# A Hyena convolution with a gated layer behind it: work that TensorE waits for at changes of stage queued earlier, and the first x * v as whole products

## Chip, core and metric

The kernel runs on one core of a Trainium2 chip. The metric is the device time of one execution in microseconds (us). The kernel before takes 3784.62 us, the median of three runs (3782.5 to 3785.52). The profile shows one further execution, with a span of 3782.9 us.

## What is computed

Four batches of 12480 positions and 128 channels. A small network makes a filter from the position embeddings; each channel of u = x * v is convolved with it by a Fourier transform of twice the length; the result times x goes through a wide layer with the gate h * cos(h).

```python
h_mlp = np.maximum(pos_emb @ w1, 0.0) @ w2
h_filt = h_mlp * np.exp(-0.01 * pos)[:, None]
u = x * v
Uf = np.fft.rfft(u, n=L, axis=1)              # L = 2 * S
Hf = np.fft.rfft(h_filt, n=L, axis=0)
y = np.fft.irfft(Uf * Hf[None, :, :], n=L, axis=1)[:, :S, :]
x = (x * y).reshape(B * S, D)                 # 49920 x 128
h = x @ w_in                                  # 128 -> 2048
out = (h * np.cos(h)) @ w_out                 # 2048 -> 128
```

## The kernel before

The Fourier transform is done as matmuls in two factors, 96 (`N1`) by 120 (`N2`). The stages of a convolution are called f1 (first factor, 64 pairs of channels), f2 (second factor, 48 units of two frequencies, with the product with the filter's spectrum), i1 and i2 (the two factors back). Batches 1 to 3 run their convolution between the matmuls of the wide layer, which fills the kernel from about 343 us on. The change concerns what comes before: the filter and the convolution of batch 0, which have TensorE to themselves.

The order of instructions on each engine is written out by hand (`manual_schedule`): each engine works through its own queue in the order in which the Python code records the instructions, and waits at the first whose inputs or buffers are not ready. Generators (`units`) record a stage in small steps; interleaving two of them with `next` sets what stands where in the queues. In `units`, `before(j)` records what unit j needs `ahead` units early, `mm` its matmuls, and `after(j)`, a generator, is stepped through while the next unit is recorded.

The stages of the first 340 us, in TensorE's order:

- The hidden layer of the filter, eleven blocks (lines 831 to 841). VectorE scales a block (`filter_scale`, L333), TensorE turns it and multiplies, ScalarE evicts. `first_u` begins here: x and v of batch 0 are loaded in 30 units, multiplied (`u_multiply`, L392), and folded into `slots` by one sum on GpSimd and one difference on VectorE (`u_sums`, L398). A unit is 104 rows by 512 numbers, multiplied in two halves of 256; `engine(j, half)` says by whom. x has three buffers and v two.
- The filter's output (`filter_out`): 30 steps of two matmuls (L354), a copy by ScalarE (L358) and two sums by VectorE (L361) into `ftile`, with `first_u` beside it.
- f1 of the filter (`f1_units` with `f1_evict_filter`): 64 matmul pairs (L404), each evicted either by ScalarE or by VectorE (L431 to L434, and the negated copies L412 and L414). `share` is the part that ScalarE takes. The remaining steps of `first_u` run beside the first part of it. Then the tables of the inverse transform are made beside it (`inverse_tables`): ten sine tables, the arguments by GpSimd (L200 to L217), the sines by ScalarE (L226), recorded up to four tables later.
- f1 of batch 0 (`f1_evict`: L420, L422, L412 and L414), in place in `slots`. Beside it eight pieces of the wide layer's input weights are converted from 64-bit numbers (`convert_units`, L133 to L156) by VectorE, ScalarE and GpSimd.
- f2 of batch 0 and of the filter together (`f2_both_units`). For each unit ScalarE and VectorE make a table w (`make_w`, L291 and L293), two buffers of which lie in the pool `both`; TensorE multiplies w with the data (L445) and with the filter (L448, L451); ScalarE scales the filter's spectrum to h (L624, three buffers); VectorE makes two products of 512 (L464) and GpSimd joins them (L471). h and w are stored to DRAM by SyncE (L626, L613) for the later batches.
- i1 (`i1_units`: L476, evicted by a ScalarE copy L484 and two VectorE sums L486). Beside it eight pieces of the output weights are converted, and six groups of a table for i2 are made and stored (`some_groups`).
- i2 with the first step of the wide layer. `next(backs[0])` records the first group of the i2 table (`make_group`, tile `tm`).

The eight PSUM banks are handed out in turn by `bank()`, so TensorE may run up to eight banks ahead of the evictions.

## Time and profile before

| part of the page or the trace | value |
|---|---|
| time, median of 3 | 3784.62 us |
| busy: TensorE, VectorE, ScalarE, GpSimd | 98%, 73%, 67%, 69% of the span |
| hidden layer of the filter | 0 to 31 us |
| filter output: TensorE; VectorE ends | 31 to 57 us; 63.1 us |
| f1 of the filter, TensorE | 63.2 to 112.7 us |
| GpSimd: last sum of u; tables | 95.8 us; 96.3 to 119.1 us |
| f1 of batch 0, TensorE | 120.6 to 164.8 us |
| f2, TensorE | 169.5 to 267.7 us |
| i1, TensorE | 271.7 to 331.7 us |
| first matmul of i2 | 336.6 us |
| TensorE busy from 345 to 3780 us | 3406.5 of 3435 us |

A line of the trace's timeline gives start, duration, engine, line of the code, operation, the tiles out and in, the number of instructions merged, and in brackets the idle time of the engine before it with what ended it. A line of the list of waits gives who waited for whom, the total, how many times and the longest. A line L201 of the kernel before is not L201 of the one after: all lines here are those of before.

### The profile page before, as it was taken

How to read it: one execution, taken by the hardware profiler on the slowest of the kernel's cores; microseconds unless marked ns; L12 is line 12 of the kernel's file. 1: busy time of each engine (PE TensorE's matmuls, PEld its weight loads, DVE VectorE, ACT ScalarE, POOL GpSimd, SP SyncE). 2: the span in 40 equal slices, each digit the busy share in tenths (PEclk: the TensorE clock that was granted, in tenths of full speed). 3: DMA queues.
4: the chain of work that ended last, by engine and by line, in shares of the span. 5: the costliest groups of instructions: out<-in, count | busy, mean ns of one | idle time of the engine just before them, and what ended most of it. 6: DMA issues, size and time to landing. Idle time of an engine off the chain costs nothing.

```text
span 3782.9 us, 47199 instructions
## 1 busy us (share of the span) xinstructions
PE 3701.9 (98%) x13546; PEld 2107.3 (56%) x13546; DVE 2762.4 (73%) x5562; ACT 2520.3 (67%) x4683; POOL 2592.6 (69%) x2342
## 2 busy tenths in 40 slices
PE   7898999999999999999999999999999999999999
PEld 6777555655466555555565556555566544444444
DVE  7887887688866777778766786788765566666666
ACT  5756776766665557666665567666664677777777
POOL 7667886588854665688745664788644577777776
PEclk9999999999999999999999999999999999999999
DMA  5263552022202650122103540122105200000000
GB/s 166 69 179 106 149 147 57 18 70 79 74 18 67 179 159 27 33 78 78 57 18 110 173 127 18 51 78 76 41 12 167 87 20 20 17 21 20 17 22 13
DMA packets 209498, 276.14 MB, mean 73 GB/s; under 512 B 17111, under 2 KB 146535, under 8 KB 209111
## 3 DMA queue, kind: packets, MB, share of 16 engines
q1 hardware_dynamic: 209239, 273.12, 24.7%
q8 instruction: 109, 1.79, 0.2%
q14 instruction: 150, 1.23, 0.1%
HBM read 193.64 MB, written 79.42 MB: 72 GB/s over the span
## 4 chain that ended last, share of the span: by engine, by line
PE 83%; POOL 6%; DVE 3%; DMA 3%; ACT 2%; issue 2%; SPq 0%; POOLq 0%; DVEq 0%; ACTq 0%
PE ph L737 32%; PE acc L762 27%; PE cv L762 5%; PE cv L501 4%; PE cv L476 4%; POOL f L746 4%; PE cv L404 3%; PE cv L445 3%; PE ph L126 2%; DMA hd<-h 2%; PE ps L404 1%; POOL tm L297 1%; DMA tm<-td 1%; DVE k L743 1%; ACT cs L751 1%
## 5 line engine op out<-in xcount | busy, mean ns | idle before, releaser
L746 POOL TENSOR_TENSOR f<-a,k 128x512 f32<-128x512 f32 (+1 forms) x1568 | 1987.4, 1268 | 1054.2 <-DVE k L743 1052.0
L737 PE MATMUL ph<-at,w_in_sb 128*128 128x512 f32 (+1 forms) x3136 | 1600.2, 592 | 5.8 <-DVE gt L753 5.2
L740 ACT ACTIVATE a<-ph,quarter 128x512 f32<-128x512 f32 (+1 forms) x1568 | 1073.4, 685 | 760.5 <-PE ph L737 751.0
L762 PE MATMUL acc<-gt,w_out_sb 128*128 128x512 f32 (+1 forms) x2688 | 1374.1, 593 | 9.7 <-ACT ot L768 9.3
L753 DVE TENSOR_TENSOR gt<-ph,cs 128x512 f32<-128x512 f32 (+1 forms) x1568 | 1077.3, 687 | 318.5 <-ACT cs L751 288.9
L743 DVE TENSOR_SCALAR k<-a 128x512 f32<-128x512 f32 (+1 forms) x1568 | 768.5, 490 | 623.4 <-ACT a L740 601.6
L751 ACT ACTIVATE cs<-f 128x512 f32<-128x512 f32 (+1 forms) x1568 | 980.3, 625 | 330.6 <-POOL f L746 328.1
L762 PEld LDWEIGHTS acc<-gt,w_out_sb 128*128 128x128 f32 x2688 | 505.6, 189 | 662.8 <-issue 619.5
L737 PEld LDWEIGHTS ph<-at,w_in_sb 128*128 128x128 f32 x3136 | 554.0, 190 | 338.7 <-issue 269.5
L471 POOL TENSOR_TENSOR slots<-slots,t 120x256 f32<-120x256 f32 x384 | 311.4, 817 | 58.7 <-DVE t L464 26.0
L501 PEld LDWEIGHTS cv<-slots,tm 96*104 96x104 f32 x1920 | 241.0, 171 | 110.7 <-issue 83.0
L501 PE MATMUL cv<-slots,tm 96*104 96x128 f32 x1920 | 255.6, 275 | 10.4 <-DVE tm L293 4.9
L762 PE MATMUL cv<-gt,w_out_sb 128*128 128x512 f32 (+1 forms) x448 | 224.5, 583 | 0.7 <-DVE gt L753 0.7
L476 PEld LDWEIGHTS cv<-cs,slots 120*96 120x96 f32 x1536 | 176.7, 167 | 67.6 <-issue 65.7
L476 PE MATMUL cv<-cs,slots 120*96 120x120 f32 x1536 | 183.1, 266 | 0.0
L445 PE MATMUL cv<-slots,w 124*120 124x256 f32 x576 | 173.0, 380 | 0.0
L445 PEld LDWEIGHTS cv<-slots,w 124*120 124x120 f32 x576 | 103.6, 184 | 123.8 <-issue 111.1
L404 PEld LDWEIGHTS cv<-c,slots 104*124 104x124 f32 x768 | 132.5, 192 | 71.2 <-issue 58.3
L404 PE MATMUL cv<-c,slots 104*124 104x192 f32 x768 | 151.2, 326 | 4.8 <-DVE gt L753 3.5
L762 PEld LDWEIGHTS cv<-gt,w_out_sb 128*128 128x128 f32 x448 | 84.9, 190 | 104.5 <-issue 99.5
L392 DVE TENSOR_TENSOR xt<-xt,vt 104x256 f32<-104x256 f32 x177 | 138.3, 788 | 0.4 <-DMA vt<-in_v_dram 0.4
L486 DVE TENSOR_TENSOR slots<-cv,other 96x240 f32<-96x240 f32 x384 | 133.7, 394 | 4.2 <-ACT other L484 4.2
(129 smaller groups left out, 2564.1 us busy)
## 6 DMA issues: line engine op xcount, KB each, us to landing
h<-hd SPq DMA_DIRECT2D x144, 240.0 KB
tm<-td SPq DMA_DIRECT2D x96, 312.0 KB
xt<-in_x_dram SPq DMA_DIRECT2D x120, 208.0 KB
vt<-in_v_dram SPq DMA_DIRECT2D x120, 208.0 KB
xs<-in_x_dram SPq DMA_DIRECT2D x120, 208.0 KB
zd<-zs SPq DMA_DIRECT2D x119, 208.0 KB
zb<-zd SPq DMA_DIRECT2D x96, 256.0 KB
w<-wd SPq DMA_DIRECT2D x144, 116.2 KB
```

Of the source, the lines that this page charges most:

```text
L404: nc.tensor.matmul(ps[0:KE, i * 2 * N1:(i + 1) * 2 * N1], u[:, b, 0:KE, i], c1[0:u.shape[0], :, :].rearrange("p r k -> p (r k)"), start=Tr ...
L445: nc.tensor.matmul(pi, w[:, i, :], parts[0:KE, :, k], start=True, stop=True)
L471: nc.gpsimd.tensor_tensor(y[:, r], y[:, r], t[:, r], op=op)
L476: nc.tensor.matmul(ps[0:N1, (i * 2 + r) * N2:(i * 2 + r + 1) * N2], parts[0:N2, r, :, b, i], cs[:, r, :], start=True, stop=True)
L501: nc.tensor.matmul(ps[0:R, i * D:(i + 1) * D], t[:, i, r, :], slots[0:N1, :, place, :], start=(r == 0), stop=(r == 1))
L737: nc.tensor.matmul(ph[:, 0:m], w_in_sb[:, c * P:(c + 1) * P], ats[n][:, 0:m], start=True, stop=True)
L740: nc.scalar.activation(a[:, 0:m], ph[:, 0:m], AF.Identity, bias=quarter[:, 0:1], scale=INV_TWO_PI)
L743: nc.vector.tensor_scalar(out=k[:, 0:m], in0=a[:, 0:m], scalar1=ROUND, scalar2=ROUND, op0=ALU.add, op1=ALU.subtract)
L746: nc.gpsimd.tensor_tensor(f[:, 0:m], a[:, 0:m], k[:, 0:m], op=ALU.subtract)
L751: nc.scalar.activation(cs[:, 0:m], f[:, 0:m], AF.Sin, scale=TWO_PI)
L753: nc.vector.tensor_tensor(gt[:, 0:m], ph[:, 0:m], cs[:, 0:m], op=ALU.mult)
L762: nc.tensor.matmul(accs[n][:, 0:m], w_out_sb[:, c, :], gt[:, 0:m], start=(c == 0), stop=(c == NFC - 1))
```

## The change

It is meant to have ready, when TensorE comes to a new stage, what that stage's first matmul needs, and to even out who does x * v of the first batch:

- x * v of batch 0: one product of 512 a unit. GpSimd does it, except for units 15, 19, 23 and 27, which VectorE does. `first_u` is a unit of two steps, not three: one from the third block of the hidden layer on, two in each three steps of the filter output, and three steps of f1 to each of the rest.
- ScalarE takes 58% of the filter's f1 evictions, not 53%.
- The tables of the inverse run on into f1 of batch 0 (`chain`), and their last four sines are recorded one by one.
- The first w of f2 is made before f1 of batch 0 goes on; the buffers of w get a pool of their own. Stores of w are recorded behind the store of h.
- The last unit of f2 joins its products on VectorE, not GpSimd.
- Conversions: one in 9 and 10 steps, not 14; the groups of tables beside i1 one in 4, not 5; the first i2 table is made before the last of the six groups.

```diff
-        t.finish(len(t.waiting))
+        while t.waiting:
+            t.finish(1)
+            yield
...
-                for half in range(2):
+                for half in (0, 1) if halves else (slice(0, 2),):
                     u_multiply(tiles[j], half, engine(j, half))
                     yield
...
-    def f2_both_units(bank):
+    def f2_both_units(bank, w_pool):
+        ws, unkept = {}, []
+        def before(j):
+            ws[j] = w_pool.tile([KE, 2, N2], F32, name="w")
+            for i in range(2):
+                make_w(ws[j][:, i, :], 2 * j + i, half=bank)
+            unkept.append(j)
...
             nc.sync.dma_start(hd[j, :, :, :, :], h[:, :, :, :])
+            while unkept:
+                k = unkept.pop(0)
+                nc.sync.dma_start(wd[k, :, :, :], ws[k][:, :, :])
+            yield from f2_product(pool, ps[0], h, 2 * j, True,
+                                  nc.vector if 2 * j + 2 == N1 else nc.gpsimd)
...
-                nc.sync.dma_start(wd[j, :, :, :], ws[j][:, :, :])
...
-        next(backs[0])
+            if g == SOME[-2]:
+                next(backs[0])
...
-                                  lambda j, half: nc.vector if half and j % 3 and j < 18
-                                  else nc.gpsimd)
+                                  lambda j, half: nc.vector if j >= 15 and j % 4 == 3
+                                  else nc.gpsimd, halves=False)
...
-                    if i >= 4:
-                        for _ in range(2):
-                            next(first_u)
+                    if i >= 2:
+                        next(first_u)
...
-                    for _ in range(1 + (j % 3 == 0)):
+                    if j % 3:
                         next(first_u)
-            f1 = f1_units(bank, ftile[0:FR, :, :, :], 0.53, f1_evict_filter)
+            f1 = f1_units(bank, ftile[0:FR, :, :, :], 0.58, f1_evict_filter)
             for _ in first_u:
-                for _ in range(2):
+                for _ in range(3):
                     next(f1)
...
-                for i, _ in enumerate(f1):
-                    if i % 5 == 0:
-                        next(sines, None)
-                for _ in sines:
-                    pass
+                first_f1 = f1_units(bank, slots[0:R, :, :, :], 0.55)
+                for i, _ in enumerate(chain(f1, first_f1)):
+                    if i % 5 == 0 and next(sines, "made") == "made":
+                        break
...
-                        if i % 14 == 0:
+                        if i % every == 0:
                             next(convert, None)
-                        elif i % 5 == 0:
+                        elif i % 4 == 1:
                             next(other, None)
...
+            w_pool = first.enter_context(tc.tile_pool(name="w", bufs=2, side="right"))
+            f2 = f2_both_units(bank, w_pool)
+            next(f2)
+            beside(first_f1, [(wind[:, c], w) for c, w in in_pieces], 9)
...
-            beside(i1_units(bank), [(w_out_sb[:, c, :], w) for c, w in out_pieces], some_groups)
+            beside(i1_units(bank), [(w_out_sb[:, c, :], w) for c, w in out_pieces], 10, some_groups)
```

## Prediction

> **What bounds the kernel now.** I read the page's slices first, then the busy time of each stage, then TensorE's waits, then the timeline at each change of stage. From 345 us on TensorE is busy 3406.5 of 3435 us, in an order that the change leaves as it is; only the convolution of the first batch, the first 340 us, can move. Here is busy time by stage (length, then PE, PEld, DVE, ACT, POOL, granted clock, DMA share, GB/s):
>
> ```profile
> 31.00:63.00 32.00, 25.84 (x120) 19.23 (x118) 29.63 (x83) 11.05 (x30) 26.84 (x32) 0.96 0.59 175
> 63.00:96.00 33.00, 31.53 (x177) 30.60 (x178) 30.64 (x95) 24.88 (x110) 29.68 (x39) 0.94 0.51 148
> 96.00:113.00 17.00, 15.14 (x83) 12.99 (x82) 16.43 (x63) 12.06 (x52) 14.06 (x39) 1.00 0.03 7
> 113.00:120.60 7.60, 0.56 (x4) 0.27 (x2) 4.69 (x17) 2.02 (x8) 5.24 (x12) 0.85 0.11 33
> 120.60:165.00 44.40, 43.99 (x252) 43.06 (x252) 38.70 (x105) 39.10 (x115) 28.76 (x31) 0.95 0.24 69
> 165.00:169.50 4.50, 0.01 (x1) 0.04 (x1) 1.66 (x6) 4.39 (x16) 0.72 (x1) 1.00 0.18 52
> 169.50:267.70 98.20, 95.87 (x480) 74.50 (x480) 83.56 (x189) 53.17 (x141) 64.28 (x91) 0.98 0.59 172
> 267.70:271.70 4.00, 0.45 (x2) 0.25 (x2) 1.83 (x3) 0.60 (x1) 3.65 (x6) 1.00 0.63 189
> 271.70:331.70 60.00, 55.58 (x510) 54.33 (x510) 45.44 (x141) 38.85 (x120) 41.31 (x54) 0.97 0.27 85
> 331.70:336.60 4.90, 0.02 (x1) 0.02 (x1) 4.69 (x16) 4.33 (x14) 3.31 (x6) 0.67 0.10 27
> ```
>
> I call them filter output (31-63), f1 of the filter (63-113), f1 of batch 0 (120.6-165), f2 (169.5-267.7) and i1 (271.7-331.7). TensorE's idle time lies between them, in waits that the list of waits names (total, times, longest):
>
> ```profile
> PE ps L404 <- ACT slots L412: 8.1, 4, 7.1
> PE ps L404 <- DVE ftile L361: 6.3, 1, 6.3
> PE cv L501 <- DVE tm L293: 4.9, 1, 4.9
> PE ps L445 <- DVE w L293: 6.4, 4, 4.7
> PE ps L476 <- POOL slots L471: 3.6, 2, 3.4
> ```
>
> These five longest waits add to 26.4 us, 0.7% of the kernel. But VectorE is 93 to 97% busy in the f1 stage of the filter, and 87% in that of batch 0 with a start that waits, so a gap can close without a stage ending sooner. The timeline shows what is behind two of them:
>
> ```profile
> 119.11 0.30 ACT L226 ACTIVATE tw_t<-turned 96x120 f32<-96x120 f32 x1 [1.89 <-POOL turned L217]
> 123.59 0.55 DVE L420 COPY slots<-ps 64x384 f32<-64x384 f32 x1 [5.75 <-PE ps L404]
> 173.23 0.59 DVE L293 SCALAR_TENSOR_TENSOR w<-even,tw_w,ps 124x120 f32<-124x120 f32 x2 [3.06 <-PE ps L448]
> 178.81 0.59 DVE L293 SCALAR_TENSOR_TENSOR w<-even,tw_w,ps 124x120 f32<-124x120 f32 x2 [0.23 <-DMA wd<-w]
> 181.45 0.24 SPq L613 DMA_DIRECT2D wd<-w  x1
> 185.29 0.59 DVE L293 SCALAR_TENSOR_TENSOR w<-even,tw_w,ps 124x120 f32<-124x120 f32 x2 [0.65 <-DMA wd<-w]
> ```
>
> The first two: ScalarE stands at the last sines, which GpSimd makes from 96.3 to 119.1; the evictions behind them keep the banks, and VectorE loses 5.75 us. The others: in f2 a new w needs its buffer's store landed. The store issued at 181.45 held w at 185.29. So the two buffers turn in about 0.6 (w) + 3.4 (store) = 4.0 us, and a unit takes 2.01 us after the first eight, which took 1.74 each.
>
> **What the Trainium skill says.** "SBUF — State Buffer", Who interferes with whom: a VectorE operation with two SBUF inputs contends with a GpSimd one that reads SBUF. The trace agrees: VectorE's sum of L398 takes 0.43 us alone, up to 0.92 beside GpSimd. "DMA: Bandwidth & Descriptors", Anatomy of one DMA: about 2 us of a DMA are fixed, mostly the receipt of the write (told there of another issue path). The 116 KB store of w landed after 3.3 us in the chain, which fits. "TensorE: Matmul & The Clock Gate", What's actually happening: the clock halves after an idle window of about 3.4 us. The first f2 unit, after 4.7 us of idling, took 3.48 us at a clock of 0.51 where later ones took 1.74.
>
> **The change, part by part.**
>
> *Hidden layer (0-31 us).* The first sum on VectorE now stands one filter block earlier and waits for x and v, which land at 19.1 us whatever the order. Blocks 6 and 7 start some 2.4 us late; with one unit on every second block the last is at about 27.4 instead of 26.8. Cost **+0.6 us**.
>
> *Filter output.* VectorE paces it. Before: 21.5 us of L361, 6.7 of sums (13), 4.8 of products (10). After: the 60 L361 at 0.37 start to start, 22.4 us, with 10 sums of 0.515, 5.2: 27.6 from a start 0.6 later. GpSimd fits: a 512-wide product, bounded by 1.41 (two halves uncontended) and 1.7 (beside VectorE), I take 1.5, and 0.97 for a sum: 2.5 us a unit against 2.75 on VectorE. End at 60.5 instead of 63.2: **-2.7 us**.
>
> *Both f1 stages.* VectorE before: 31 filter evictions at 1.35 (41.9), 13 sums at 0.71 (9.2), 2 products (1.5), then 29 evictions of batch 0 at 1.23 (35.7) and eight conversions at 1.0: 96.3 us. After: 27 at 1.35 (36.5), 16 sums (11.4), four whole products between 0.7 and 1.2, taken as 1.0 (4.0), 35.7, 8.0, and 0.6 for the first w: 96.2. No difference in work. What goes is the stall: the ten sines are spread over 37 yields of the filter and 34 of batch 0, 1.8 us apart, where GpSimd needs 1.8 to 2.2 us for each and is up to four ahead: **-5.75 us**, less some 1.3 of new waits for the last sines and for v (a load of v has 3.1 us of GpSimd work to hide in and needs 3.3). ScalarE takes four evictions more (4.7 us); it was free there.
>
> *First w early.* VectorE ended at 166.3 and ScalarE at 168.6 before, and w came after both. With w ready and conversions ending earlier, f2 starts when the later engine is done, by VectorE's sum 166.3 - 2.7 - 5.75 + 1.3 = 159.2; ScalarE's larger share makes it 160. So f2 starts at **160 instead of 169.5: -9.5 us** for everything so far. An idle of some 4 us stays: the last seven banks are evicted at 0.58 each.
>
> *Stores of w behind the store of h.* The added wait. Two buffers are as before, but w(0) is now stored only after h(0): SyncE issues the store of h(0) 0.4 us after the end of unit 0, that of w(0) 0.35 later, and it lands 3.3 to 3.9 us after that. w(2) on VectorE waits for it, so unit 2 starts about 5.0 us after the end of unit 0 (before: 1.74), and both products of unit 0 queue behind w(2). Then the ring turns at the same 2.01. Before, eight fast units took up part of the difference: unit 8 stood 12.7 us after unit 0; now 5.0 + 6 x 2.03 = 17.2. **+4.5 us**, between 2 (a warm clock, a fast store) and 6. In the steady part the order of the two stores only makes that of h one unit fresher: nothing.
>
> *Last product of f2 by VectorE.* Before: TensorE ended at 267.7 and i1 ran from 271.7. After: 0.4 for h (no late store before it), 1.3 for the products, two sums at 0.4: 2.6 us. **-1.4 us.**
>
> *i1.* Conversions and tables move forward, but VectorE's sum (64 x 0.65 + 8 x (1.0 + 1.1 of stall) = 58) is the same and it ends last. Only the first time table leaves the end: 0.4, and perhaps 1 us of clock after a shorter idle: **-1.1 us.**
>
> Sum: -9.5 + 4.5 - 1.4 - 1.1 = -7.5; I round up to **-8**, as the filter's f1 also starts after 3 us of idling instead of 6.3, at a better clock: 3784.6 - 8 = **3776.6 us**.
>
> **The rivals.**
> *A, as above: 3774 to 3780.* For it: VectorE's sums. Chance 0.5; 0.3 of it lies beyond -7.6 us.
> *B, the waits simply go: 3770.* The store of w(0) lands early or its late start is made up, as h no longer waits for its own stores (36.8 us of such waits before): -7.5 - 4.5 - 2 = -14. Against it: the two-buffer ring of w, on which the store of h has no hold. Chance 0.27.
> *C, GpSimd or ScalarE becomes the bound: 3782.* GpSimd carries 26 whole products at 1.5 to 1.7 and 30 sums, VectorE stands behind each product in order, and ScalarE meets the last sines late: 4 to 6 us of the gain are lost. GpSimd is at 84 to 90% already. Chance 0.17.
> *D, slower: 3792.* The store of w behind that of h lands 0.4 us later in each turn: 46 units x 0.2 = +9, with the +4.5 and a gain of only 6: +7.5. Against it: SyncE waited 40.9 us for w in f2 and 7.6 for h, so h is ready first. Chance 0.06.
>
> **How the numbers follow.** Predicted: A, 3776.6. The range leaves out the outer part of B and of D: 3769 to 3783. Faster by over 0.2% (under 3777.0): 0.3 + 0.27 = 0.57. Within 0.2%: 0.2 of A, 0.17, 0.01 of D: 0.38. Slower: 0.05.
>
> **What would show it.** Right: f2's first matmul near 160 us; no wait of 7 us on L412's evictions; a new wait of about 3 us of VectorE's third w on the store of w, then units of 2.01; i1 2.6 us after f2; everything after 345 us as it was. Wrong: units of f2 at 1.74 throughout (the ring was not the bound); an f2 that starts later than 164 (VectorE stood behind GpSimd's products); or a changed time after the first 340 us.

## The result, and the profile after

The kernel after takes **3797.82 us** (median; 3795.11 to 3798.57), that before 3783.56 us beside it: 14.3 us more, a ratio of 1.0036 with a 95% interval of 1.0019 to 1.0053. The prediction said 3776.6, in a range of 3769 to 3783, and faster: the result lies outside the range, on the slower side. The profiled execution has a span of 3795.6 us.

From here on line numbers are those of the kernel after, which stand 1 to 10 higher than those of before (L404 is L407, L445 is L448, L476 is L479); views of the kernel before and of runs built on it (e5, e6, e8, e9, e15, e16) keep the lines of before. From the first step of the wide layer on nothing is lost: the first matmul of f1 of batch 1 stands at 627.5 us instead of 613.7, 13.8 later, and the end is 12.7 later. So the loss lies where the change is. The stages of after (length, then busy time of PE, PEld, DVE, ACT, POOL, granted clock, DMA share, GB/s), cut at the same events as in the table of before:

```profile
31.00:61.00 30.00, 26.28 (x121) 19.68 (x122) 27.60 (x70) 11.50 (x31) 23.01 (x24) 0.98 0.52 146
61.00:103.00 42.00, 38.80 (x217) 37.63 (x217) 39.78 (x116) 34.86 (x155) 26.52 (x28) 0.93 0.52 147
103.00:127.00 24.00, 17.69 (x96) 15.39 (x96) 18.08 (x59) 15.46 (x60) 19.26 (x50) 1.00 0.05 12
127.00:173.00 46.00, 38.27 (x201) 34.36 (x202) 37.81 (x97) 36.81 (x110) 30.70 (x32) 0.96 0.26 74
172.00:277.00 105.00, 97.86 (x480) 75.39 (x480) 83.31 (x187) 54.12 (x143) 64.17 (x91) 0.97 0.55 163
277.00:280.00 3.00, 0.33 (x3) 0.18 (x2) 2.87 (x6) 0.60 (x1) 2.47 (x4) 1.00 0.63 186
280.00:354.00 74.00, 59.20 (x512) 57.31 (x511) 53.40 (x155) 44.59 (x135) 47.08 (x60) 0.93 0.28 83
```

The gaps between stages are shorter, as meant: 3.1 us ahead of the filter's f1 (6.3 before), 3.6 ahead of f2 (4.7), 2.7 ahead of i1 (3.4), 1.3 ahead of i2 (4.9). But the stages are longer: f2 105 us instead of 98, i1 74 instead of 60, with no engine near its full time in i1. TensorE's waits in the first 400 us (total, times, longest) show it:

```profile
PE ps L479 <- DVE slots L489: 14.3, 8, 2.7
PE ps L407 <- ACT slots L415: 7.6, 7, 2.7
PE ps L448 <- DVE w L296: 6.2, 6, 4.0
PE ps L407 <- DVE slots L417: 5.3, 7, 1.2
...
PE ps L448 <- ACT slots L415: 3.6, 1, 3.6
PE ps L407 <- DVE ftile L364: 3.1, 1, 3.1
PE ps L479 <- POOL slots L474: 2.7, 1, 2.7
PE cv L504 <- DVE slots L489: 1.3, 1, 1.3
```

The top line, 14.3 us of waits for evictions inside i1, stood at 4.4 in before. Inside f1 the one wait of 7.1 us at the last sines has become fourteen of at most 2.7, adding to more (12.9 against 10.2).

| point | before | predicted | after |
|---|---|---|---|
| first matmul of the filter's f1 | 63.2 | 60.5 | 60.8 |
| last sine of the tables | 119.1 | - | 126.4 |
| first matmul of f2 | 169.5 | 160 | 172.5 |
| f2, to the start of its last matmul | 98 | +4.5 | 104 |
| first of f2 to first of i1 | 101.5 | 104.6 | 107.4 |
| first of i1 to first of i2 | 65.5 | about 64.5 | 75.0 |
| first of i2 to f1 of batch 1 | 277.2 | as before | 272.7 |

Three losses, +3.0 us up to f2, +5.9 in f2, +9.4 in i1, and 4.5 regained in i2 make +13.8. The prediction expected -9.5 of the first, so most of what failed lies there and in i1. The regained part is put down to the clock: TensorE begins i2 after 1.3 us of idling, not 4.9. The first ten microseconds of i2, of before and then of after (the column ahead of the last two is the clock):

```profile
336.00:346.00 10.00, 8.83 (x36) 7.75 (x37) 2.64 (x7) 4.70 (x12) 2.73 (x5) 0.50 0.68 193
```

```profile
354.00:364.00 10.00, 7.96 (x52) 6.22 (x53) 4.00 (x9) 5.38 (x12) 3.48 (x5) 1.00 0.31 87
```

At half the clock TensorE did 36 matmuls, at the full one 52 in less busy time. In e8 (below), where the table of i2 stands as in before but TensorE idles for only 2.7 us ahead of i2, the clock of the first ten microseconds is 0.83 and 3.2 us are regained.

**Ahead of f2.** GpSimd ends its last sum of u at 102.2 instead of 95.8; its tables, the loads behind their stores, and the conversions follow 7 us late. It isn't short of time for x * v: from 61 to 103 us it is busy for 26.5 of 42 us, where in before it was for 29.7 of the 33 us from 63 to 96. It stands for VectorE's four whole products (9.7 us in four waits) and for loads of v (2.7 us). Two of the four waits:

```profile
64.62 0.73 POOL L401 TENSOR_TENSOR slots<-xt 104x256 f32<-104x256 f32 x1 [2.85 <-DVE xt L395]
96.59 0.73 POOL L401 TENSOR_TENSOR slots<-xt 104x256 f32<-104x256 f32 x1 [3.29 <-DVE xt L395]
```

VectorE is busy for 39.8 of these 42 us, and the new order puts more ahead of the end of u: some 93 steps of the filter's f1 are recorded beside the rest of `first_u`, where before had 70 (counted from the code).

Then eight conversions have to fit. After's timeline of GpSimd and VectorE in f1 of batch 0 (start, duration, engine, line, what, idle time before):

```profile
133.60 1.08 POOL L136 TENSOR_SCALAR power<-power 128x256 uint32<-128x256 uint32 x1 [7.22 <-DVE power L134]
134.76 1.09 POOL L138 TENSOR_SCALAR power<-power 128x256 uint32<-128x256 uint32 x1
135.93 0.96 POOL L148 TENSOR_TENSOR sig<-sig,low 128x256 f32<-128x256 f32 x1
136.97 0.86 POOL L157 TENSOR_TENSOR power<-sig,power 128x256 f32<-128x256 f32 x1
137.80 1.08 POOL L136 TENSOR_SCALAR power<-power 128x256 uint32<-128x256 uint32 x1
...
144.36 0.42 DVE L152 SCALAR_TENSOR_TENSOR power<-raw,power 128x256 uint32<-128x256 uint32 x1 [1.01 <-POOL power L138]
```

A piece takes GpSimd 4.2 us (133.60 to 137.80), and in after it works them off all but without a pause from 133.6 to 167.3. Between two pieces stand four to five pairs, of which VectorE evicts about two; five times it reaches the join of a piece (L152) before GpSimd has made its exponents (L138), 2.9 us in all, and the evictions behind it in VectorE's queue wait too. ScalarE stands six times for VectorE's part of a piece (L142), 5.4 us in all. In before the first piece started at 127.35, one came each 4.55 to 5.8 us, and VectorE was the one that was waited for:

```profile
132.08 0.85 POOL L156 TENSOR_TENSOR power<-sig,power 128x256 f32<-128x256 f32 x1 [1.68 <-DVE power L151]
```

**In f2.** The new wait is where the prediction put it:

```profile
172.71 0.62 DVE L296 SCALAR_TENSOR_TENSOR w<-even,tw_w,ps 124x120 f32<-124x120 f32 x2 [1.91 <-ACT ps L294]
176.80 0.34 SPq L628 DMA_DIRECT2D hd<-h  x1
177.19 5.06 SPq L631 DMA_DIRECT2D wd<-w  x3
181.38 0.59 DVE L296 SCALAR_TENSOR_TENSOR w<-even,tw_w,ps 124x120 f32<-124x120 f32 x2 [8.05 <-DMA wd<-w]
181.87 0.67 PE L448 MATMUL ps<-slots,w 124*120 124x256 f32 x2 [4.04 <-DVE w L296]
182.98 1.05 PE L448 MATMUL ps<-slots,w 124*120 124x256 f32 x2
```

The store of the first w is issued at 177.19, behind that of h; VectorE stands 8.05 us at the third w, TensorE 4.04 us. After those the clock is at half: the last line takes 1.05 us where 0.59 is usual. "TensorE: Matmul & The Clock Gate" in the Trainium skill, What's actually happening, has the clock halve after some 3.4 us without work; the gaps of 4.0 here and of 4.9 ahead of i2 in before agree, and so does the gap of 2.7 ahead of i1 in after, behind which the clock stayed at 1.00. The length of one gap doesn't settle it, though: within i1 of after the clock fell to 0.50 behind gaps of 2.16 and 2.69 us (next part).

**In i1.** TensorE's timeline in after:

```profile
279.86 10.30 PE L479 MATMUL ps<-cs,slots 120*96 120x120 f32 x96 [2.67 <-POOL slots L474]
291.31 4.32 PE L479 MATMUL ps<-cs,slots 120*96 120x120 f32 x40 [1.16 <-DVE slots L489]
296.64 4.46 PE L479 MATMUL ps<-cs,slots 120*96 120x120 f32 x40 [1.01 <-DVE slots L489]
303.38 4.32 PE L479 MATMUL ps<-cs,slots 120*96 120x120 f32 x40 [2.27 <-DVE slots L489]
308.81 4.47 PE L479 MATMUL ps<-cs,slots 120*96 120x120 f32 x40 [1.12 <-DVE slots L489]
315.43 10.08 PE L479 MATMUL ps<-cs,slots 120*96 120x120 f32 x80 [2.16 <-DVE slots L489]
...
337.49 16.04 PE L479 MATMUL ps<-cs,slots 120*96 120x120 f32 x128 [2.69 <-DVE slots L489]
```

Five pairs (40 matmuls) for each piece, then a wait, 5.3 to 5.4 and 6.6 to 6.7 us apart by turns. The 128 matmuls that end the stage have no further piece beside them and run without a stop. But the clock fell twice in the stage, behind the waits of 2.16 and 2.69 us (the column ahead of the last two):

```profile
317.00:319.00 2.00, 2.00 (x12) 2.00 (x11) 1.63 (x6) 0.42 (x3) 1.05 (x2) 0.50 0.00 0
339.00:341.00 2.00, 2.00 (x12) 2.00 (x12) 2.00 (x7) 1.73 (x7) 1.76 (x3) 0.50 0.03 8
```

So 80 matmuls took 10.08 us where 40 take 4.32, and the last 128 took 16.04 where e11 (below) needs 14.16 for 136: some 4 us together. In before the pieces reached over nearly all of i1 and cost 0.7 to 1.4 us of waiting each:

```profile
303.51 5.96 PE L476 MATMUL ps<-cs,slots 120*96 120x120 f32 x56 [1.39 <-DVE slots L486]
310.15 5.96 PE L476 MATMUL ps<-cs,slots 120*96 120x120 f32 x56 [0.69 <-DVE slots L486]
```

### The profile page after: what moved, and what is told of

It is laid out like the page before. It is cut to its first block, busy times and chain, and to the rows that moved or that the text cites. A ratio compares the mean times of both kernels' runs of the same rounds, so it can differ in the third digit from the quotient of the medians.

```text
span 3795.6 us, 47120 instructions
## 1 busy us (share of the span) xinstructions
PE 3706.4 (98%) x13546; PEld 2108.2 (56%) x13546; DVE 2771.2 (73%) x5536; ACT 2519.9 (66%) x4703; POOL 2583.6 (68%) x2318
## 4 chain that ended last, share of the span: by engine, by line
PE 81%; POOL 6%; DVE 3%; DMA 2%; ACT 2%; issue 2%; SPq 0%; POOLq 0%; DVEq 0%; ACTq 0%
PE ph L747 31%; PE acc L772 27%; PE cv L772 5%; PE cv L504 4%; PE cv L479 4%; POOL f L756 4%; PE cv L407 3%; PE cv L448 3%; PE ph L127 2%; PE ps L448 1%; ACT cs L761 1%; POOL tm L300 1%; DMA wd<-w 1%; DVE k L753 1%; DMA tm<-td 1%
## 5 line engine op out<-in xcount | busy, mean ns | idle before, releaser
L753 DVE TENSOR_SCALAR k<-a 128x512 f32<-128x512 f32 (+1 forms) x1568 | 776.4, 495 | 611.6 <-ACT a L750 592.2
L479 PEld LDWEIGHTS cv<-cs,slots 120*96 120x96 f32 x1536 | 176.7, 167 | 67.6 <-issue 65.7
L479 PE MATMUL cv<-cs,slots 120*96 120x120 f32 x1536 | 183.1, 266 | 0.0
L448 PE MATMUL cv<-slots,w 124*120 124x256 f32 x576 | 173.0, 380 | 0.0
L448 PEld LDWEIGHTS cv<-slots,w 124*120 124x120 f32 x576 | 103.6, 184 | 123.8 <-issue 111.1
L407 PEld LDWEIGHTS cv<-c,slots 104*124 104x124 f32 x768 | 132.5, 192 | 71.2 <-issue 58.3
L407 PE MATMUL cv<-c,slots 104*124 104x192 f32 x768 | 151.2, 326 | 4.8 <-DVE gt L763 3.5
L489 DVE TENSOR_TENSOR slots<-cv,other 96x240 f32<-96x240 f32 x384 | 133.6, 394 | 4.2 <-ACT other L487 4.2
L395 DVE TENSOR_TENSOR xt<-xt,vt 104x256 f32<-104x256 f32 (+1 forms) x169 | 133.9, 800 | 0.9 <-DMA vt<-in_v_dram 0.9
```

What stands on the lines that cost most here:

```text
L407: nc.tensor.matmul(ps[0:KE, i * 2 * N1:(i + 1) * 2 * N1], u[:, b, 0:KE, i], c1[0:u.shape[0], :, :].rearrange("p r k -> p (r k)"), start=Tr ...
L448: nc.tensor.matmul(pi, w[:, i, :], parts[0:KE, :, k], start=True, stop=True)
L479: nc.tensor.matmul(ps[0:N1, (i * 2 + r) * N2:(i * 2 + r + 1) * N2], parts[0:N2, r, :, b, i], cs[:, r, :], start=True, stop=True)
L753: nc.vector.tensor_scalar(out=k[:, 0:m], in0=a[:, 0:m], scalar1=ROUND, scalar2=ROUND, op0=ALU.add, op1=ALU.subtract)
```

## The experiments

I held three theories. **1**: the conversions stand too close, GpSimd and the in-order queues behind it bind. **2**: the late stores of w cost. **3**: x * v by GpSimd puts everything behind it late. The first matmul of the filter's f1 moves by up to 2 us between executions of the same code, so I read stages from one first matmul to the next:

| kernel | time, ratio to before (95%) | filter's f1 starts | to f2 | f2 to i1 | i1 to i2 |
|---|---|---|---|---|---|
| before | 3783.56 | 63.2 | 106.3 | 101.5 | 65.5 |
| after | 1.0036 (1.0019 to 1.0053) | 60.8 | 111.7 | 107.4 | 75.0 |
| e1_i1_spacing | 1.0029 (1.0018 to 1.0041) | 60.5 | 111.9 | 106.9 | 67.8 |
| e2_w_stores | 1.0018 (1.001 to 1.0027) | 60.4 | 114.5 | 100.5 | 73.5 |
| e3_x_times_v | 1.004 (1.0026 to 1.0053) | 64.5 | 111.8 | 109.0 | 74.4 |
| e4_tables | 1.0042 (1.0029 to 1.0054) | 62.0 | 111.7 | 107.6 | 75.4 |
| e5_w_last | 1.0004 (0.9995 to 1.0012) | 64.4 | 107.5 | 100.4 | 65.1 |
| e6_u_alone | 1.0009 (1.0001 to 1.0017) | 61.9 | 115.3 | 101.2 | 65.0 |
| e7_i1_and_w | 1.0015 (1.0009 to 1.0022) | 62.6 | 110.8 | 100.6 | 67.8 |
| e8_spacing_alone | 1.0022 (1.0014 to 1.0031) | 64.6 | 111.5 | 101.4 | 70.1 |
| e9_five_halves | 1.0046 (1.0033 to 1.0058) | 64.3 | 107.9 | 117.9 | 66.2 |
| e10_five_halves_after | 1.0077 (1.0063 to 1.0091) | 61.5 | 110.8 | 120.3 | 74.2 |
| e11_tables_5 | 3798.73 (one run) | 61.2 | 110.0 | 107.5 | 69.6 |
| e12_halves_and_chain | 1.0037 (1.0023 to 1.0051) | 63.5 | 103.2 | 117.3 | 66.2 |
| e13_best | 0.9996 (0.9988 to 1.0004) | 63.5 | 104.3 | 102.4 | 65.7 |
| e14_new_u | 1.0005 (0.9997 to 1.0013) | 60.5 | 105.8 | 105.4 | 65.3 |
| e15_h2_w3 | 3792.11 (one run) | 65.4 | 107.9 | 105.2 | 65.9 |
| e16_no_w_stores | 3771.28 (one run) | 63.7 | 105.9 | 89.1 | 65.5 |
| e17_w_made_again | 1.0207 (1.0192 to 1.0222) | 63.8 | 104.6 | 89.2 | 65.2 |
| e18_half_made_again | 1.0094 (1.0077 to 1.0111) | 63.8 | 104.6 | 92.8 | 65.2 |

The way to f2 scatters most: the kernels with after's code up to there (after, e1, e2, e7, e10, e11) have 110.0 to 114.5, those with before's (before, e9, e15, e16) 105.9 to 107.9. In that column only 4 us or more count.

### One part of the change undone

```diff
-            beside(i1_units(bank), [(w_out_sb[:, c, :], w) for c, w in out_pieces], 10, some_groups)
+            beside(i1_units(bank), [(w_out_sb[:, c, :], w) for c, w in out_pieces], 14, some_groups, (5, 0))
```

> The kernel after, but beside i1 a conversion stands once in 14 steps and a table step once in 5, as before; the last table of i2 stays ahead of the sixth group. Theory 1 (GpSimd and the in-order queues: the conversions stand closer together than GpSimd can work them off, and the evictions of i1 stand behind each piece): i1 falls from 73.7 us (first to last start of a matmul) to 60 to 62, the seven waits of 1.1 to 2.7 us of L479 on L489 shrink under 1 us, and the time falls by 9 to 13 us to 3785 to 3789 (part of it may be lost again at the start of i2). Theory 2 (the stores of w behind the store of h are what costs): i1 isn't concerned and the time stays within 2 us of 3797.8. Theory 3 (x * v by GpSimd makes everything behind it late): the same, within 2 us.

Theory 1 for i1: 67.8 us instead of 75.0, 64 of them to its last matmul, a little more than expected. The median time, 3794.24, is only 3.6 under after's, not the 9 to 13 expected; the span of the profile by 6.2. Part is given back at i2, which starts after 3.8 us of idling again, not 1.3.

```diff
         def before(j):
+            while unkept:
+                k = unkept.pop(0)
+                nc.sync.dma_start(wd[k, :, :, :], ws[k][:, :, :])
...
-            unkept.append(j)
+            if j == 0:
+                unkept.append(j)
+            else:
+                nc.sync.dma_start(wd[j, :, :, :], ws[j][:, :, :])
```

> The kernel after, but w is stored again as soon as it is made (w(0) when f2 begins to record w(1)); all else as after. Theory 2 (stores of w behind the store of h): the first w's stores leave ahead of h's, the third w waits less, f2 falls from 104.2 us (first to last start of a matmul) to 98 to 100, and the time falls by 4 to 6 us to 3792 to 3794. Theory 1 (GpSimd and the spacing): f2's length is set by its ring of two w buffers in either order, so f2 changes by under 2 us and the time stays over 3795.5.

Theory 2: f2 to i1 takes 100.5 us, 6.9 less than in after, and the time is 3790.05, 7.8 less, more than the 4 to 6 expected. Here the clock fell only once in f2.

```diff
-                                  lambda j, half: nc.vector if j >= 15 and j % 4 == 3
-                                  else nc.gpsimd, halves=False)
+                                  lambda j, half: nc.vector if half and j % 3 and j < 18
+                                  else nc.gpsimd)
...
-            f1 = f1_units(bank, ftile[0:FR, :, :, :], 0.58, f1_evict_filter)
+            f1 = f1_units(bank, ftile[0:FR, :, :, :], 0.53, f1_evict_filter)
```

> The kernel after, but x * v of batch 0 in halves, with VectorE's share, the places in the queues and ScalarE's share of evictions (0.53) as before. Theory 3 (GpSimd, given more of x * v, ends it at 103 instead of 96 us, so its tables, the loads behind their stores and the conversions all come 7 us later): GpSimd ends u at 95 to 97, the last sine falls from 126.4 to 119 to 121, the conversions start by 128, f2 starts at 163 to 167 instead of 172.5, and the time falls by 5 to 9 us to 3789 to 3793. Theory 1 in its strict form (only the spacing of the conversions matters): the filter output takes its 2.7 us longer again, f2 starts within 3 us of 172.5, and the time stays within 3 us of 3797.8.

A miss for theory 3 as I had it; the strict form of theory 1 fits. The last sine does move to 121.4, 56.9 us after the start of the filter's f1 instead of 65.6, but f2 starts no sooner (111.8), and the filter's output takes its 3 us again: 3797.91. The conversions, still one in 9 steps, began sooner and cost the same: VectorE waited five times, 4.6 us, for GpSimd's L138.

```diff
-                for i, _ in enumerate(chain(f1, first_f1)):
-                    if i % 5 == 0 and next(sines, "made") == "made":
-                        break
+                for i, _ in enumerate(f1):
+                    if i % 5 == 0:
+                        next(sines, None)
+                for _ in sines:
+                    pass
...
-            beside(first_f1, [(wind[:, c], w) for c, w in in_pieces], 9)
+            beside(first_f1, [(wind[:, c], w) for c, w in in_pieces], 14)
```

> The kernel after, but the tables are recorded within the filter's f1 with the last four sines at its end, as before, and beside f1 of batch 0 a conversion stands once in 14 steps; x * v, the first w and i1 as after. Theory 1 (what costs in f1 of batch 0 is that conversions in 96 steps once in 9 are denser than GpSimd works, and sines spread among its evictions hold ScalarE): f2 starts at 163 to 167 instead of 172.5 and the time falls by 5 to 9 us. Theory 3 (x * v late on GpSimd): the tables still end at 126, now with one stall of TensorE of 10 to 13 us in place of several; the conversions still come late; f2 starts at 170 to 178 and the time is 3796 to 3803.

Theory 3's figure: 111.7, nothing gained. The waits only changed form, one of 10.9 us at the last sines, and after it 232 matmuls without a break:

```profile
127.99 41.77 PE L407 MATMUL ps<-c,slots 104*124 104x192 f32 x232 [10.90 <-DVE w L296]
173.70 0.70 PE L448 MATMUL ps<-slots,w 124*120 124x256 f32 x2 [3.94 <-ACT slots L415]
```

With one conversion in 14 steps, then, f1 of batch 0 has no breaks; but this run also took back the spread of the sines, and with x * v as in after their stall is long. Neither undoing made f2 start sooner, and that called for single parts on the kernel before.

### One part alone

```diff
             w_pool = first.enter_context(tc.tile_pool(name="w", bufs=2, side="right"))
             f2 = f2_both_units(bank, w_pool)
             next(f2)
             beside(f1_units(bank, slots[0:R, :, :, :], 0.55),
...
             yield from f2_product(pool, ps[0], h, 2 * j, True,
                                   nc.vector if 2 * j + 2 == N1 else nc.gpsimd)
```

> The kernel before with two parts alone: the first w made ahead of f1 of batch 0 (its buffers in a pool of their own, the stores of w ahead of those of h as before), and the last product of f2 joined by VectorE. Theory 1 (each of these two parts gains what it removes, and what made the kernel after slower lies elsewhere): f2 starts 1 to 3 us sooner than at 169.5 (the wait of 4.7 us for w becomes one of 2.6 to 3.6 us for the last evictions), i1 starts 1 us sooner behind f2's end; i1 and the rest as before; 2 to 4 us faster than before, 3779 to 3781. Rival (the first w in the middle of the evictions costs as much there, since ScalarE and VectorE have to turn to each other, or the wait only moves): f1 of batch 0 ends later by what the gap loses, within 1 us of before.

The rival: no gain (1.0004). The wait of 4.7 us for w became one of 4.0 for the last evictions, and the wait at the last sines grew from 7.1 to 8.2, as the terms of the first w now stand behind them in ScalarE's queue. The last product did shorten the way to i1, by some 1 us.

```diff
-                                  lambda j, half: nc.vector if half and j % 3 and j < 18
-                                  else nc.gpsimd)
+                                  lambda j, half: nc.vector if j >= 15 and j % 4 == 3
+                                  else nc.gpsimd, halves=False)
```

> The kernel before with the new x * v of batch 0 alone (whole products, GpSimd's share, its places in the queues, 58% of the filter's evictions by ScalarE). Theory 3 (GpSimd ends x * v 6 to 7 us later and all that hangs on its tables comes as much later): the filter's f1 starts at 60.5 as in the kernel after, but the last sine comes at 125 to 127, the wait of 7 us at it grows to 11 to 14, the conversions start 6 us later, f2 starts at 174 to 177 instead of 169.5, and the time is 4 to 8 us over before. Rival (x * v gains the 2.7 us of the filter output and costs nothing): f2 starts at 166 to 167, 2 to 3 us faster than before.

Theory 3 holds here, where the sines stand at the end of the filter's f1: f2 starts at 177.2, the wait at the last sines is 11.8 us, and x * v as in after costs 9.0 us up to f2 against a start 1.3 us sooner. The time is 4.8 us over before's, at the low end of what was expected. As in after, GpSimd waits for VectorE's products (11.5 us in four waits) and for loads of v (4.4 us from 61 to 105 us); the engine of a product, whole products and the place in the queues go together in this edit, and no run parts them.

> The kernel after with both undone, the spacing beside i1 and the late stores of w. If the two causes add: the time falls by what they gave one by one, 3 to 5 and 6 to 8 us, together 9 to 13, to 3785 to 3789, with f2 of 98 us and i1 of 62 to 65 us from first to last matmul; what is left over before, 2 to 6 us, is then in what leads up to f2 (172 to 175 instead of 169.5) and in the table of i2 made within i1. If they hide each other (i1 starts when f2 ends, so an i1 that is set by its tables and loads would not move with it): 3789 to 3792.

(The edits of e1 and e2 together.) The two add within 2 us: 3788.16, 9.7 us under after, f2 and i1 each as in the run that undid it alone. Left are 5 to 6 us over before, all on the way to f2 and in i1's last table of i2, which stands within i1 now: 67.8 us against 65.0 to 65.6 with the same spacing in before, e5 and e6.

```diff
-                        if i % 14 == 0:
+                        if i % every == 0:
                             next(convert, None)
-                        elif i % 5 == 0:
+                        elif i % 4 == 1:
                             next(other, None)
```

> The kernel before with the denser conversions alone (one in 9 steps beside f1 of batch 0, one in 10 beside i1, table steps one in 4). Theory 1 (VectorE and ScalarE stand at each piece for one another and for GpSimd; spread out, the eight banks hide that, packed they don't, and the pairs behind the last piece then run at TensorE's pace with VectorE idle): i1 grows from 60.4 to 68 to 73 us, f1 of batch 0 ends 2 to 5 us later, the gap ahead of i2 stays at 4 to 5 us; 9 to 15 us slower than before, 3792 to 3798. Rival (the slow i1 of the kernel after comes of the i2 table made within it and of loads that land late behind the stores of w): i1 stays under 63 us and the time within 2 us of before.

Theory 1: 8.6 us over before from the spacing alone (9 beside f1, 10 beside i1), just under the 9 to 15 expected, 5.2 on the way to f2 and 4.5 up to i2. On the way to f2 VectorE waited seven times for L137 (L138 in after), 2.5 us in all, and ScalarE seven times for VectorE's L141, 5.3 us.

### The stores of f2, and the two spacings beside i1

```diff
-                ws[j] = pool.tile([KE, 2, N2], F32, name="w")
+                ws[j] = Halves()
                 for i in range(2):
+                    ws[j].append(pool.tile([KE, N2], F32, name="w", bufs=5))
                     make_w(ws[j][:, i, :], 2 * j + i, half=bank)
-                nc.sync.dma_start(wd[j, :, :, :], ws[j][:, :, :])
+                    nc.sync.dma_start(wd[j, :, i, :], ws[j][:, i, :])
```

> The kernel before, but w of f2 lies in five buffers of half a unit in place of two of a whole one, each half stored by itself (58 KB, still ahead of the store of h); all else as before. Theory 2 in its strict form (f2 is set by the ring of w: 0.6 us to make it and 3.4 for its store, over two units, 2.01 us a unit): over two and a half units the ring would allow 1.6, TensorE needs 1.74 and VectorE 1.74 to 1.8, so f2 falls from 98 us to 86 to 90, the waits of VectorE on stores of w vanish, and the time falls by 8 to 12 us to 3770 to 3775. Rival (f2 is set by something else in the turn, the banks or VectorE standing for ScalarE's terms, or the DMA queues, which have a half more stores to carry): f2 stays at 95 to 99 us and the time within 3 us of before.

> The kernel after, but w in five buffers of half a unit, each stored by itself, still behind the store of h. Theory 2 (the late stores cost because the third w stands for the landing of the first store, then TensorE's clock falls, then the ring of two holds every later unit): the first wait moves to the second half of the third w and stays at 3 to 6 us, the later units go at 1.74 to 1.85; f2 falls from 104.5 us to 90 to 94 and the time by 10 to 14 us, to 3784 to 3788. Rival (the later units are set by something other than the ring): f2 stays over 100 us and the time over 3795.

Both missed far: f2 to i1 grew to 117.9 and 120.3 us. Halving the buffers halved the rows of the stores to 480 bytes. In the steady part of f2 the queues moved 153 GB/s where before they moved 179, at nearly the same busy share (57% and 61%), and in the chain of waits a store of half a w took 5.2 to 5.9 us where one of a whole w had taken 3.3 to 4.1. A store of h, the same size as ever, took 5.1 to 6.2 us instead of 3.5 to 4.2. More buffers were paid for with slower stores, so the two runs say nothing on the ring; they do say that f2 hangs on its stores. Whether the short rows do it or the doubled number of stores of w wasn't parted.

> The kernel after, but beside i1 the steps of the tables stand once in 5 steps, as before; conversions stay at one in 10. It parts the two spacings beside i1, which were undone together. If the conversions' spacing is the cause (each piece makes VectorE and ScalarE wait for each other): i1, from its first matmul to the first of i2, stays at 73 to 75 us, with gaps of TensorE of 1 to 2.5 us. If the tables' spacing is (GpSimd over 90% busy with sums of tables and conversions): it falls to 68 to 70 us.

This parts the two spacings that e1 undid together (its edit: one in 10 kept, tables at 5). i1 takes 69.6 us to the first of i2, the case of the tables; its matmuls take 62 us, with the clock at 1.00 throughout. TensorE's timeline:

```profile
294.38 4.32 PE L479 MATMUL ps<-cs,slots 120*96 120x120 f32 x40 [1.00 <-DVE slots L489]
299.76 4.32 PE L479 MATMUL ps<-cs,slots 120*96 120x120 f32 x40 [1.07 <-DVE slots L489]
305.15 4.32 PE L479 MATMUL ps<-cs,slots 120*96 120x120 f32 x40 [1.06 <-DVE slots L489]
```

A piece comes every 5.38 us: five pairs and one conversion on VectorE, with a wait of 1.1 us for ScalarE behind each conversion. In after two pieces took 12.06 us, 6.03 each. What came to it there is the second table step, with GpSimd's sums:

```profile
298.27 2.37 POOL L300 TENSOR_TENSOR some<-some,spare 96x208 f32<-96x208 f32 x3
300.60 0.72 POOL L157 TENSOR_TENSOR w_out_sb<-sig,power 128x256 f32<-128x256 f32 x1
...
312.66 0.72 POOL L157 TENSOR_TENSOR w_out_sb<-sig,power 128x256 f32<-128x256 f32 x1
```

In 10 steps GpSimd has 3.7 us of conversion and two or three sums of tables by turns. With three sums (0.79 us each here, 0.62 otherwise) it works for 6.0 us without a pause; with two it waits 0.95 us for ScalarE and VectorE. It had 8.7 to 9.4 us of work in each 10 between 290 and 330 us; ScalarE, which has a part in each table step too, had 5.8 to 7.3. In e11 only one table step falls between two pieces (5 and 10 share every second step), so GpSimd has 4.4 us; but half the tables are then left for after i1, TensorE waits 7.5 us for i2's first table, and the whole gains nothing (3798.73).

Two more things of i1 stand in the lists. In after the first table step stands at step 1 and not 5, ahead of the landing of its loads, and the evictions stand behind it in ScalarE's queue:

```profile
284.70 0.47 ACT L294 ACTIVATE some<-rows,tw_t 96x208 f32<-96x208 f32 x1 [6.88 <-DMA tw_t<-twd]
```

(0.4 us in e1.) And VectorE's own conversion got slower, although VectorE nowhere waits for GpSimd in i1: groups of VectorE in i1 (busy, mean ns, idle before), after and then e11:

```profile
L142 DVE TENSOR_SCALAR sig<-raw 128x256 uint32<-128x256 uint32 x8 | 5.6, 699 | 0.0
```

```profile
L142 DVE TENSOR_SCALAR sig<-raw 128x256 uint32<-128x256 uint32 x8 | 2.3, 282 | 0.0
```

Three of after's eight took 1.39 to 1.40 us, each begun while GpSimd was at the last of three sums; the join ahead of them (L152) took 0.57 to 0.68 us, not 0.41. Such a piece is the one that takes 1.3 us more than the next. e2, e3, e4 and e8, all with table steps at 4 and pieces at 10, have the same three. With both spacings as before, one operation of 1.40 us is left (before, e1, e7), and none in e11. Why it lasts longer there isn't shown.

> The kernel before with w in five half buffers and with the inverse tables running on into f1 of batch 0, their last four sines one by one; x * v, the spacing of the conversions (one in 14, over the 124 steps that remain) and all else as before. It tells what spreading the sines is worth where GpSimd isn't late. If the stall of 5.75 us of VectorE at the last sines is simply freed, as the prediction had it: f2 starts 3 to 5 us sooner than with five halves alone. If it only breaks up into shorter waits, since GpSimd makes a table in 1.8 to 2.2 us and ends them at the same time: f2 starts within 1.5 us of where it starts with five halves alone, and the time is within 1.5 us of that kernel's.

(e9 with the tables run on, as in after; x * v and spacing as before.) f2 is slow as in e9, but it starts 103.2 us after the filter's f1, 4.7 sooner than in e9 and 2.7 sooner than the best of the kernels with before's code up to there: where u ends as early as in before and the conversions aren't dense, spreading the sines frees a good part of the stall.

### Putting together

> The kernel after without its costly parts: x * v of batch 0, both spacings (one in 14, tables one in 5), the place of the last i2 table and the order of the stores of w as before. What stays of the change: tables run on into f1 of batch 0, the first w made ahead, the last product of f2 by VectorE. If these gain what they removed (4 to 5 us by the tables as in the run with halves and chain, 0 to 1 by the first w, 1 by the last product): f2 starts 103 to 104.5 us after the start of the filter's f1 (before: 106.3), f2 98, i1 as before, 3776 to 3779, 4 to 6 us faster than before. If the tables' gain was an effect of that run alone: 3781 to 3784.

(The kernel after with the edits of e1, e2 and e3, one conversion in 14 beside f1, and the last i2 table at the end.) The profile shows the gain, f2 at 167.8, batch 1 at 609.5 us instead of 613.7, a span of 3779.4. The times don't confirm it: 3781.27 against 3782.48, a ratio of 0.9996 (0.9988 to 1.0004), within the range of the second case. It is no slower than before, and not shown to be faster.

```diff
-            beside(first_f1, [(wind[:, c], w) for c, w in in_pieces], 9)
+            beside(first_f1, [(wind[:, c], w) for c, w in in_pieces], 12)
```

> As the run before it, but x * v as in the kernel after, and conversions beside f1 of batch 0 one in 12 (101 steps are left there behind the tables, and nine calls must fit). Theory 3 (x * v late on GpSimd keeps f2 late, whatever the spacing): f2 starts 110 to 112 us after the start of the filter's f1, as in the kernel after with 111.7, less 2.5 for the sooner start of that; 3781 to 3786. Theory 1 (the spacing of 9 was it): f2 starts 105 to 107 us after, and the time is 3776 to 3779.

Theory 1 has it on the way to f2: with x * v as in after, and only the conversions wider, f2 starts after 105.8 us (111.7 in after), at 166.3. TensorE's timeline in e14:

```profile
124.65 31.53 PE L407 MATMUL ps<-c,slots 104*124 104x192 f32 x172 [1.93 <-ACT slots L415]
166.35 1.21 PE L448 MATMUL ps<-slots,w 124*120 124x256 f32 x2 [5.01 <-ACT slots L415]
```

172 matmuls run without a break, where after, behind its first 104, had a wait at each further piece. But f2 then takes 105.4 us although w is stored as in before: the conversions end late, SyncE issues the store of the first w only at 170.96, behind their last stores, and VectorE waits 6.75 us for it. The same wait as in after, through another queue. Read with e3 and e13, which have x * v as in before, it says more: where the sines run on, as in after, f2 starts after 111.7 (after) and 111.8 us (e3) with one conversion in 9, whichever x * v it is, and after 105.8 (e14, one in 12) and 104.3 us (e13, one in 14) with them wider. So in after it is the spacing that costs. Of the differences of 5.9 and 7.5 us, 2.4 stand already at the last sine, where the code doesn't differ yet, so 3.5 to 5.1 us are the least that is shown. The time of e14 is that of before, 1.0005 (0.9997 to 1.0013), not the 3776 to 3779 expected under this theory.

```diff
-                h = pool.tile([N2, 2, CB, 4], F32, name="h", bufs=3)
+                h = pool.tile([N2, 2, CB, 4], F32, name="h", bufs=2)
```

> The kernel before, but f2 with three whole buffers of w in place of two and two of h in place of three (the size of the stores unchanged). If the ring of w sets the 2.01 us of a unit and h's store has no hold: f2 falls from 98 us to 86 to 90. If h's ring sets it (the chain of waits in f2 of before goes over the stores of h for 63%): with two buffers f2 grows to 100 to 125 us, ScalarE waiting for the store at each h. If the traffic of both sets it: 96 to 100.

(With three buffers of w.) f2 to its last matmul takes 100.5 us, where the second and the third case meet. VectorE no longer waits for a store of w; ScalarE waits for those of h, from 190 to 262 us, as long as in before (32.2 us):

```profile
ACT h L624 <- DMA hd<-h: 33.2, 34, 1.4
```

> The kernel before, but only the first w of f2 is stored; the later batches load that one for every unit (their transforms are computed with the wrong table; the traffic of the loads is the same). A w then waits for no store, and h's stores have the queues alone. If the ring of w sets the unit: f2 falls from 98 us to 86 to 90. If that of h does, and its store takes the 3.6 us whatever lies beside it: f2 stays at 95 to 98 us. If the store of h gets faster without w's: 87 to 92, with ScalarE's waits for stores of h down from 32 us to under 10.

86.3 us, and no wait for a store of h is left, in a kernel that leaves out 47 of the 48 stores of w. Together with e15 this says that it isn't the ring of w alone: with both kinds of stores in the queues a unit takes 2.0 to 2.1 us, with two buffers of w or with two of h, and without w's stores 1.7 to 1.8. No run has three of both, so the ring of h and the traffic aren't parted here.

> The version without the costly parts (tables run on, first w ahead, last product by VectorE), and w isn't stored at all: batches 1 to 3 make it again, by ScalarE and VectorE, where they loaded it (144 units of some 0.62 and 0.59 us beside the matmuls of the wide layer). If f2 pays for the stores of w: f2 falls from 98 to 85 to 88 us, and if the later work lies beside TensorE's, which is busy throughout from 345 us on, the time is 11 to 14 us under before, 3769 to 3772. Rival (in the later batches ScalarE and VectorE stand for each other at each w and TensorE waits): f2 as short, but the part after 345 us grows by 5 to 30 us, and the time is at or over before.

> The same, but only every second w is stored and loaded, the others are made again. If the traffic of the stores of w and h together sets the unit of f2, half of w's is enough to bring it near TensorE's 1.74: f2 of 86 to 91 us, 3770 to 3775. If w's ring sets it, a w that is stored holds one of the two buffers as long as before and each second unit waits: f2 of 90 to 96 us. Later cost: half that of the run with all.

```diff
                 ws[j] = pool.tile([KE, 2, N2], F32, name="w")
-                nc.sync.dma_start(ws[j][:, :, :], wd[j, :, :, :])
+                for i in range(2):
+                    make_w(ws[j][:, i, :], 2 * j + i)
```

With all work done f2 takes 86.7 us, and 90.1 with half of w's stores (99.7 in e13). The 90.1 is nearer to the 86.7 than to the 99.7, which speaks for the traffic, but it lies where the two expectations meet. The rest of the kernel pays: 3862.54 and 3819.4 us, 78 and 35 over before. From 345 to 3780 us TensorE's waits for VectorE's gate (gt) grew from 5.2 to 40.8 and 24.6 us. So the work of making w again wasn't free beside the wide layer, though VectorE is busy only 74 to 75% of that stretch. No version that does all the work is shown to beat before.

## Why the prediction was wrong

1. **Hidden layer and filter output: right.** The filter's f1 starts at 60.8, against 60.5; over all runs with this part 60.4 to 62.6, without it 63.2 to 65.4. The better clock behind the shorter gap, for which the sum was rounded up, didn't come: it is 0.50 at the start of the filter's f1 in both kernels, up to 65 us at least.
2. **"Both f1 stages": wrong, and the largest miss.** The step added up VectorE's work, found it equal, and took the stall of 5.75 us as freed, less 1.3. But it left GpSimd out of f1 of batch 0: eight pieces of 4.2 us each. By e13's pace there (244 matmuls, four a pair, in 44.08 us) nine steps pass in an estimated 3.3 us, twelve in 4.3 and fourteen in 5.1, so at one in 9 the pieces come faster than GpSimd works. Spread to one in 12 the same kernel starts f2 5.9 us sooner (e14), and with x * v as before the wide and the close spacing stand 7.5 us apart (e13, e3). The stall was freed only in part: with the sines spread and nothing close, f2 starts after 103.2 to 104.6 us (e12, e13, e17, e18), with before's code after 105.9 to 107.9. x * v, put forward as theory 3, isn't shown to cost anything where the sines are spread (e14, e3); where they are not, it costs 9 us alone (e6), since u ends later and one wait at the last sines grows with it. That is why e4, which undid the spread together with the spacing, gained nothing.
3. **"First w early": no gain shown.** The 4.7 us ahead of f2 were mostly the last evictions, 4.0 of them left in e5 and 3.6 in after.
4. **Stores of w behind h: mechanism right, size short.** +4.5 was said, +5.9 measured up to i1 and 6.9 undone by e2. Unit 2 started 5.9 us after the end of unit 0 (175.93 to 181.87), not 5.0, VectorE's third w waited 8.05 us where about 3 was said, and the second fall of the clock in the same stage wasn't counted. What was wrong was the aside that the store of h has no hold on a unit: in e15, with three buffers of w and two of h, a unit still takes 2.0 to 2.1 us and ScalarE waits for h's stores. The chain of waits in f2 of before had it, with the stores of h first, and so had the list of waits, whose 36.8 us the prediction names under B; I had gone by VectorE and SyncE:

```profile
by line: DMA hd<-h 63.1%; DMA wd<-w 10.9%; PE ps L445 7.4%; ACT h L624 6.6%; DVE w L293 4.2%; PE ps L451 2.7%; PE ps L448 2.5%; issue 2.5%; DVE t L464 0.7%; DVE slots L464 0.6%; ACT ps L291 0.6%; ACTq L624 0.3%; SPq L613 0.2%; DVEq L293 0.2
```

5. **Last product by VectorE: right.** TensorE waits 2.7 us, 2.6 was said. To the first matmul of i1 that is 0.7 us less than before, not 1.4, since before's first two matmuls of i1 ran at 271.0, ahead of the 271.7 that was counted from.
6. **"i1 equal": wrong.** -1.1 was said, +9.4 measured. Again VectorE's sum was taken as unchanged and GpSimd's work for a piece wasn't asked. With table steps at 4 and pieces at 10, GpSimd has no pause in every second piece, and there VectorE's L142 took 1.40 us instead of 0.28: the sum was wrong in a duration it took as fixed. In before a piece had 6.6 to 7.6 us; with the tables at 5 the slow operations are gone (e11), and with both spacings undone 7.2 us come back (e1). Three more terms weren't in the sum: two falls of the clock within the stage (some 4 us), the first table step ahead of its load (6.9 us of ScalarE), and the table of i2 within i1 (some 2 us, e1 and e7). They overlap, and how the 9.4 divides among them wasn't measured.

Rival C had part of the mechanism, an engine other than VectorE that becomes the bound with VectorE standing behind it in order. But it blamed the products, and sized the loss at 4 to 6 us; e3 takes the products back and gains nothing. The size of step 2's and step 6's loss wasn't in any case that I priced. One effect went the other way: behind the earlier table of i2 TensorE's clock stayed up, and 4.5 us came back in i2. The parts measured alone, +4.8 (e6), +8.6 (e8) and +7.8 (undone by e2), add to 21, not 14. Two things lie between: that clock, and e6's loss, most of which is gone where the sines are spread (e14). How the 7 us part between them was not measured.

## What to carry to other kernels

Work put beside a stage has a rate as well as a sum: before setting it closer, divide what each engine has to do for one piece by the time in which the stage passes that many steps, for the engines with slack too. A sum of one engine's work takes its durations as fixed; here a VectorE operation took five times as long beside a GpSimd without pauses. In-order queues turn an engine that is late by a microsecond into waits of the engines that evict. An undoing that takes back two parts at once, as e4 did, doesn't say which of them cost, so test parts alone as well as undone. A shorter gap between stages is worth its idle time only if what fed the gap doesn't come later: a store moved behind another may hold a two-buffer ring and let the clock fall a second time.

## What of the hardware was unexpected

- A 128x256 uint32 operation of VectorE took 0.28 us in e11 and 1.40 us in three of eight cases in after, e2, e3, e4 and e8, with GpSimd over 87% busy beside it in after. Which of GpSimd's operations does it wasn't tried.
- TensorE's clock fell to half behind gaps of 2.16 and 2.69 us within i1 of after, and stayed at 1.00 behind one of 2.67 us ahead of i1.
- The same bytes of w stored in rows of 480 instead of 960 bytes, in twice as many stores: 153 instead of 179 GB/s, and f2 longer by 16 us (e9).
- Without the stores of w, those of h held nobody: ScalarE's waits for them, 32.2 us in before from 190 to 262 us, went to none (e16).
